# The steps that split the weights, dealt out in four rows over the units of the second batch

## The chip, the cores and the metric

The kernel runs on one core of one Trainium2 chip, as one launch. The metric is the device time of the whole launch in microseconds, as a median of several runs. TensorE does the matmuls and writes to PSUM; ScalarE (ACT), VectorE (DVE) and GpSimd (POOL) do the elementwise work; SyncE (SP) starts nearly all transfers.

## What is computed

Two blocks in a row, all in float32. First a polynomial attention: with two small sketches S1 and S2, every query and key of length 32 becomes 64 products (features), and a feature map takes the place of the softmax. Then a feed-forward block with a gate, over 4352 tokens of width 128 and a hidden width of 1536.

```
a, b    = S1 @ x, S2 @ x                  # 8 numbers each
phi(x)  = all 64 products a_i * b_j       # for q and for k
kv, z   = sum_s phi(k) v,  sum_s phi(k)   # per batch and head
attn    = (phi(q) @ kv) / (phi(q) @ z + 1e-6)
x       = attn, as (4 * 1088 tokens, 4 heads * 32)
out     = (silu(x @ w_gate) * (x @ w_val)) @ w_out
```

## The kernel before

**Blocks and units.** There are four batches of 1088 tokens. Each is cut into three blocks, of 384, 384 and 320 tokens, which gives twelve blocks. The hidden width is cut into twelve slices of 128. A *unit* is one slice for one block: a matmul with a slice of w_gate, a matmul with the slice of w_val, the silu of the first, and its product with the second, which goes to a slot of `hbuf`. Two units later, `down` (L949) multiplies that slot with a slice of w_out and adds it up in PSUM.

**The loop.** The first batch is worked through with hand-written code. The other three run in one loop over y from 0 to 107 near the end of the kernel: nine blocks of twelve units. The second batch is y = 0 to 35. Within a step of the loop the order of issue is: the unit, up to two `down`, then one piece (or two) of the attention work for a later batch (`parts_of`, from the generator `attentions`), then one step of the splitting of the weights (`next(cutting, None)`), then perhaps a step of the splitting of the tokens. No scheduler reorders this: every engine takes its instructions in the order of issue, and waits on semaphores hold the order of data. At y = 12, 36 and 60 a `group` of small matmuls of the attention stands ahead of the unit.

**Plain and split units.** For y up to 37, `unit` uses plain float32 matmuls (L918); each shows as two records in the trace. Later units (`cut_unit`) use three float32r matmuls in the place of one float32 matmul. For them the weights and the tokens have to be split first. For w_val the parts are used from y = 38 on, for w_gate from y = 48 on.

**What the splitting does.** A weight array (wv or wg) is split in four pieces of 128 x 384, and each piece takes four steps, all recorded under L841:

- w1, on ScalarE: the weight, scaled by a little less than one and rounded to float32r
- low, on GpSimd: the weight less w1, in a tile of the tag `sgl`, of which there are six buffers
- wb, on ScalarE: low, times 4096 and rounded
- wd, on GpSimd: w1 less wb

In the profile, the w1 and wb of wg carry the name graw, its wd the name gphq, after the buffers that they use.

**The order before.** `cut_weights` sets the steps of piece c at 3c, 3c + 1, 3c + 3 and 3c + 4, and hands out one such position at each unit, from y = 3 on; it goes on with wg when wv is done. So the ScalarE step wb is issued two units after the GpSimd step low that it reads, followed by the w1 of the next piece. ScalarE has the silu of each unit (L924) in the same queue.

**GpSimd's other work.** In the second batch GpSimd also adds up the key features (`feature_sums`, L526, tile zs): four additions in a row, once for each later batch. They are read at the next group, by small matmuls (L679).

**PSUM.** Units take three banks in turn (g0, g1, g2), two for each unit. The matmul for w_val of a unit takes the bank that held the gate of the unit before, which that unit's silu sets free. The matmul for w_gate takes the bank of the value of two units before, which DVE's product (L935) sets free.

Of the kernel before, what the change touches and what calls it, by code (L numbers as in the profile page):

```python
# [2 lines left out]

# [10 lines left out]
AF = mybir.ActivationFunctionType  # L14
# [6 lines left out]
def kernel(  # L21
# [28 lines left out]
    nc = tc.nc  # L50
# [17 lines left out]
    steps = [(sum(plan[:s]), n) for s, n in enumerate(plan)]  # L68
# [32 lines left out]
    def hold(*tags):  # L101
        for t in tags:
            held.update((place[t], place[t] + 1) if t in "ab" else (place[t],))
# [31 lines left out]
    wg = const.tile([P, NCH, P], FP32, name="wg")  # L135
    wv = const.tile([P, NCH, P], FP32, name="wv")
# [33 lines left out]
    def load_next():  # L170
# [36 lines left out]
        out=ident[:], in_=ident[:], pattern=[[-1, P]], base=0, channel_multiplier=1,  # L207
# [79 lines left out]
    def run(*gens):  # L287
        for g in gens:
            for _ in g:
                pass  # L290
# [521 lines left out]
    BETA = 4096.0  # L812
    CUT = 1.0 - 2.0**-13
# [3 lines left out]
    def whole(ap):  # L817
        return ap.bitcast(FP32)

    def homes(w):  # L820


        if w is wv:
            for c in range(4):
                yield [
                    stage.tile([P, 3, P], F32R, tag=tag, name=name, bufs=6)[:]
                    for tag, name in (("exp", "w1"), ("man", "wb"), (("exp", "man")[c % 2], "wd"))
                ]
        else:
            big = lambda pool, tag, bufs: pool.tile([P, 2, 3, P], F32R, tag=tag, name="g" + tag, bufs=bufs)  # L830
            for c in range(2):
                t = [big(stage, "raw", NRAW), big(stage, "raw", NRAW), big(apool, "phq", 2)]
                for k in range(2):
                    yield [x[:, k] for x in t]

    def cut_weights(w):

        steps = {}

        def put(at, f, **args):  # L840
            steps.setdefault(at, []).append(lambda: f(**args))  # L841

        for c, (w1, wb, wd) in enumerate(homes(w)):
            src = w[:, 3 * c : 3 * c + 3, :]
            low = fpool.tile([P, 3, P], FP32, tag="sgl", name="low", bufs=6)[:]
            w_parts[id(w), c] = (w1, wb, wd)
            sub = dict(op=ALU.subtract)
            put(3 * c, nc.scalar.activation, out=w1, in_=src, func=AF.Copy, scale=CUT)
            put(3 * c + 1, nc.gpsimd.tensor_tensor, out=low, in0=src, in1=whole(w1), **sub)
            put(3 * c + 3, nc.scalar.activation, out=wb, in_=low, func=AF.Copy, scale=BETA)  # L850
            put(3 * c + 4, nc.gpsimd.tensor_tensor, out=wd, in0=whole(w1), in1=whole(wb), **sub)
        for at in sorted(steps):
            for step in steps[at]:
                step()
            yield

    def cut_tokens(i, engine=nc.gpsimd):

        t0, n = blocks[i]
        x = xT[:, t0 : t0 + n]  # L860
        x1, x0, xd = x_parts[i] = [
            apool.tile([P, BW], F32R, tag=tag, name=name, bufs=2)
            for tag, name in (("qb", "x1"), ("dT", "x0"), ("rd", "xd"))
        ]
        nc.scalar.activation(x1[:, 0:n], x, AF.Copy, scale=CUT)
        engine.tensor_tensor(
            out=x0[:, 0:n], in0=x, in1=whole(x1[:, 0:n]), op=ALU.subtract
        )
        yield
        nc.vector.scalar_tensor_tensor(  # L870
            out=xd[:, 0:n], in0=whole(x0[:, 0:n]), scalar=-BETA, in1=whole(x1[:, 0:n]),
            op0=ALU.mult, op1=ALU.add,
        )

    def cut_unit(i, j, both=False):

        t0, n = blocks[i]
        x1, x0, xd = (x[:, 0:n] for x in x_parts[i])
        ws = (wg, wv) if both else (wv,)
        parts = [[x[:, j % 3, :] for x in w_parts[id(w), j // 3]] for w in ws]  # L880
        ds = [bank()[:, 0:n] for _ in ws]
        g = None if both else bank()[:, 0:n]
        for d, (_, _, wd) in zip(ds, parts):
            nc.tensor.matmul(d, wd, xd, start=True, stop=True)  # L884
        if not both:
            nc.tensor.matmul(g, wg[:, j, :], xT[:, t0 : t0 + n], start=True, stop=True)  # L886
        ps = []
        for w1, wb, _ in parts:
            p = bank()[:, 0:n]
            nc.tensor.matmul(p, w1, x1, start=True, stop=False)  # L890
            nc.tensor.matmul(p, wb, x0, start=False, stop=True)  # L891
            ps.append(p)
        sums = []
        for d in ds:
            s = fpool.tile([P, BW], FP32, tag="sgl", name="sum", bufs=6)[:, 0:n]
            nc.scalar.activation(s, d, AF.Copy, scale=-1.0 / BETA)  # L896
            sums.append(s)
        for p, s in zip(ps, sums):
            nc.vector.scalar_tensor_tensor(  # L899
                out=s, in0=p, scalar=1.0 + 1.0 / BETA, in1=s, op0=ALU.mult, op1=ALU.add  # L900
            )
        sg = fpool.tile([P, BW], FP32, tag="sg", name="sg", bufs=3)[:, 0:n]
        nc.scalar.activation(sg, sums[0] if both else g, AF.Silu)  # L903
        slot_of[i, j] = slots.pop(0)
        hj = hbuf[:, slot_of[i, j], :]
        hidden[i, j] = hj
        todo.append((i, j))
        nc.gpsimd.tensor_tensor(out=hj[:, 0:n], in0=sg, in1=sums[-1], op=ALU.mult)  # L908

    def unit(i, j, late=False, between=(None, None)):  # L910


        t0, n = blocks[i]
        g, u = bank(), bank()
        for o, w in ((g, wg), (u, wv)):
            if between[0] and w is wv:
                between[0]()
            nc.tensor.matmul(  # L918
                o[:, 0:n], w[:, j, :], xT[:, t0 : t0 + n], start=True, stop=True
            )  # L920
        sg = fpool.tile(
            [P, BW], FP32, tag="sgl" if late else "sg", name="sg", bufs=6 if late else 3
        )
        nc.scalar.activation(sg[:, 0:n], g[:, 0:n], AF.Silu)  # L924
        slot_of[i, j] = slots.pop(0)
        hj = hbuf[:, slot_of[i, j], :]
        hidden[i, j] = hj
        todo.append((i, j))
        if late:
            if between[1]:  # L930
                between[1]()
            nc.scalar.copy(hj[:, 0:n], u[:, 0:n])
            lates.append((hj[:, 0:n], sg[:, 0:n]))
        else:
            nc.vector.tensor_tensor(  # L935
                out=hj[:, 0:n], in0=sg[:, 0:n], in1=u[:, 0:n], op=ALU.mult
            )
# [5 lines left out]
    def down():  # L943

        i, j = todo.pop(0)
        n = SPLIT if i == LAST else blocks[i][1]
        if j == 0:
            acc[i] = bank("g1" if i == 1 else "acc")
        nc.tensor.matmul(  # L949
            acc[i][:, 0:n],  # L950
            wo[:, j, :],
            hidden[i, j][:, 0:n],
            start=(j == 0),
            stop=(j == NCH - 1),
        )
        if i != LAST:
            hidden.pop((i, j))
            slots.append(slot_of[i, j])
        if j == NCH - 1:
            store(i, n)  # L960
# [47 lines left out]
    for h in range(H):  # L1008
# [13 lines left out]
        out=s12[:, 0:H, :, :],  # L1022
        in0=sTv.unsqueeze(1).to_broadcast([P, H, 2, R]),
        in1=own[:].unsqueeze(2).unsqueeze(3).to_broadcast([P, H, 2, R]),
# [75 lines left out]
    def group():  # L1100
        while ahead[0] != "pe":
            ahead[0] = next(att)
        ahead[0] = next(att, "end")
# [32 lines left out]
    w = ("wg", "wv")  # L1136
# [43 lines left out]
    END = len(line) * NCH  # L1180
    PLAIN, VALUE = 3 * NCH + 2, 4 * NCH
    coming_x = iter(())
    cutting = chain(*(cut_weights(w) for w in (wv, wg)))
    for y in range(END):
        i, j = line[y // NCH], y % NCH
        if y in (NCH, 3 * NCH, 5 * NCH):
            group()
        if y == 3 * NCH:
            oldest[0] = True
            hold("acc")  # L1190
            run(cut_tokens(i, nc.vector))
        if y < PLAIN or y == END - 1:
            unit(i, j)
        else:
            cut_unit(i, j, both=y >= VALUE)
        lag = LAG if y < PLAIN else min(5, END - y + 1)
        for _ in range(2):
            if len(todo) > lag:
                down()
        parts_of(2 if y in (0, 4, 6, 7, 8) else 1)  # L1200
        if 3 <= y:
            next(cutting, None)
        if j == 4 and 3 * NCH < y < END - NCH:
            coming_x = cut_tokens(line[y // NCH + 1])
        if j in (4, 6):
            next(coming_x, None)
# [43 lines left out]
```

## Time and profile before

The median of three runs is 304.58 us (304.5 to 305.13). The profiled execution spans 303.4 us.

| engine | busy us | share of the span | instructions |
|---|---|---|---|
| TensorE, matmul | 288.4 | 95% | 2307 |
| TensorE, weight load | 206.1 | 68% | 2307 |
| VectorE | 200.4 | 66% | 400 |
| ScalarE | 154.6 | 51% | 369 |
| GpSimd | 127.8 | 42% | 144 |

The second batch runs from about 92 to 176 us. The rows of the table are totals over stages with different limits, so what a stage is limited by has to be read from its own waits. A wait is printed as "engine, what it writes, line <- the engine and line that released it". In a timeline the bracket after a row holds the idle time ahead of it and what ended that. "Granted clock" is the share of full speed that TensorE was given in a stretch.

The L841 steps in the trace:

| step | engine | count | mean us | first and last start, us |
|---|---|---|---|---|
| w1 of wv | ScalarE | 4 | 0.51 | 98.1, 117.7 |
| low of wv | GpSimd | 4 | 1.00 | 98.7, 118.8 |
| wb of wv | ScalarE | 4 | 0.52 | 102.0, 119.8 |
| wd of wv | GpSimd | 4 | 1.00 | 102.6, 120.4 |
| w1 of wg | ScalarE | 4 | 0.51 | 130.4, 146.7 |
| low of wg | GpSimd | 4 | 0.99 | 131.0, 147.9 |
| wb of wg | ScalarE | 4 | 0.52 | 134.2, 151.3 |
| wd of wg | GpSimd | 4 | 1.00 | 141.7, 151.9 |

### The profile page before, as it was taken

The page shows a single profiled execution, that of the slowest core. Times are in us where ns is not written, and L with a number is a line of the kernel's source. Part 1 is how long each engine was busy: PE and PEld are TensorE (multiplying, and loading weights), DVE is VectorE, ACT ScalarE, POOL GpSimd, SP SyncE. Part 2 cuts the span into 40 slices and gives each one's busy share as a digit, 9 for nine tenths or more (in the row PEclk, how much of TensorE's full clock was granted, in tenths as well). Part 3 has the DMA queues.
Part 4 walks back from the last instruction along what each step waited for, and adds up shares of the span by engine and source line. Part 5 has one row for each costly group of instructions (what it writes and reads, how often), then busy time and mean ns, then how long its engine had stood idle before and what let it go on. Part 6 is the DMA issues. An engine that isn't in the chain of part 4 may idle for free.

```text
span 303.4 us, 6168 instructions
## 1 busy us (share of the span) xinstructions
PE 288.4 (95%) x2307; PEld 206.1 (68%) x2307; DVE 200.4 (66%) x400; ACT 154.6 (51%) x369; POOL 127.8 (42%) x144
## 2 busy tenths in 40 slices
PE   8899999999999993996899999999999999999995
PEld 7545566657665541753567767787778888888985
DVE  4997988692536982165688348998657666676751
ACT  3566764422103422341422236567868888888870
POOL 3216222174000348029510006777547575576660
PEclk9999999999999996999799999999999999999999
DMA  7554490414411000050001001001001010010101
GB/s 195 161 184 106 123 306 0 149 23 154 101 28 22 0 3 0 22 108 0 0 0 27 3 15 35 0 2 26 0 2 28 2 17 5 0 29 1 23 2 26
DMA packets 26142, 14.63 MB, mean 48 GB/s; under 512 B 18688, under 2 KB 24192, under 8 KB 26112
## 3 DMA queue, kind: packets, MB, share of 16 engines
q1 hardware_dynamic: 25456, 14.13, 18.3%
q8 instruction: 18, 0.29, 0.4%
q10 hardware_dynamic: 656, 0.10, 0.2%
q14 instruction: 12, 0.10, 0.1%
HBM read 11.41 MB, written 2.23 MB: 45 GB/s over the span
## 4 chain that ended last, share of the span: by engine, by line
PE 86%; POOL 5%; DVE 3%; ACT 2%; issue 1%; DMA 1%; SPq 0%; DVEq 0%; POOLq 0%
PE PS L918 29%; PE PS L949 26%; PE PS L884 6%; PE PS L890 6%; PE PS L891 6%; POOL zs L526 4%; PE PS L886 2%; PE PS L771 2%; PE PS L333 2%; PE PS L367 1%; DMA kld<-in_k_dram 1%; PE PS L321 1%; DVE sum L899 1%; PE PS L964 1%; POOL low L841 1%
## 5 line engine op out<-in xcount | busy, mean ns | idle before, releaser
L949 PE MATMUL PS<-hbuf,wo 128*128 128x384 f32 (+2 forms) x288 | 105.9, 464 | 0.4 <-DVE o L978 0.4
L908 POOL TENSOR_TENSOR hbuf<-sg,sum 128x384 f32<-128x384 f32 (+1 forms) x69 | 69.8, 1014 | 67.6 <-ACT sum L896 32.2
L899 DVE SCALAR_TENSOR_TENSOR sum<-PS,sum 128x384 f32<-128x384 f32 (+1 forms) x128 | 62.6, 526 | 29.5 <-ACT sum L896 27.2
L924 ACT ACTIVATE sg<-PS 128x384 f32<-128x384 f32 (+1 forms) x75 | 35.1, 472 | 66.0 <-PE PS L918 62.2
L918 PE MATMUL PS<-xT,wv 128*128 128x384 f32 (+1 forms) x150 | 59.9, 482 | 9.2 <-ACT sg L924 8.9
L949 PEld LDWEIGHTS PS<-hbuf,wo 128*128 128x128 f32 x288 | 53.1, 191 | 18.2 <-issue 1.9
L935 DVE TENSOR_TENSOR hbuf<-sg,PS 128x384 f32<-128x384 f32 (+1 forms) x69 | 36.2, 525 | 40.6 <-PE PS L918 27.7
L918 PE MATMUL PS<-xT,wg 128*128 128x384 f32 (+1 forms) x150 | 59.8, 481 | 0.0
L896 ACT ACTIVATE sum<-PS 128x384 f32<-128x384 f32 (+1 forms) x128 | 53.4, 465 | 5.6 <-PE PS L884 5.2
L918 PEld LDWEIGHTS PS<-xT,wv 128*128 128x128 f32 x150 | 28.6, 194 | 27.9 <-ACT sg L924 10.7
L918 PEld LDWEIGHTS PS<-xT,wg 128*128 128x128 f32 x150 | 27.8, 192 | 18.4 <-issue 1.5
L903 ACT ACTIVATE sg<-sum 128x384 f32<-128x384 f32 (+1 forms) x59 | 29.7, 503 | 17.0 <-DVE sum L899 16.3
L884 PE MATMUL PS<-xd,gphq 128*128 128x384 f32 (+1 forms) x59 | 34.6, 587 | 0.0
L890 PE MATMUL PS<-x,w 128*128 128x384 f32 (+1 forms) x69 | 25.4, 369 | 0.0
L884 PE MATMUL PS<-xd,wd 128*128 128x384 f32 (+1 forms) x69 | 24.7, 357 | 0.0
L891 PE MATMUL PS<-x,wb 128*128 128x384 f32 (+1 forms) x69 | 22.6, 328 | 0.0
L890 PE MATMUL PS<-x,graw 128*128 128x384 f32 (+1 forms) x59 | 19.2, 325 | 0.0
L891 PE MATMUL PS<-x,graw 128*128 128x384 f32 (+1 forms) x59 | 19.1, 324 | 0.0
L884 PEld LDWEIGHTS PS<-xd,wd 128*128 128x128 f32 x69 | 13.1, 190 | 6.8
L884 PEld LDWEIGHTS PS<-xd,gphq 128*128 128x128 f32 x59 | 11.1, 189 | 6.4 <-issue 0.4
L841 POOL TENSOR_TENSOR low<-wv,w 128x384 f32<-128x384 f32 x4 | 4.0, 996 | 27.1 <-ACT w L841 27.1
L890 PEld LDWEIGHTS PS<-x,w 128*128 128x128 f32 x69 | 13.0, 188 | 1.6 <-ACT xT L788 0.3
(129 smaller groups left out, 330.6 us busy)
## 6 DMA issues: line engine op xcount, KB each, us to landing
kld<-in_k_dram SPq DMA_DIRECT2D x4, 544.0 KB, 4.1
vld<-in_v_dram SPq DMA_DIRECT2D x12, 144.0 KB, 5.0
qld<-in_q_dram SPq DMA_DIRECT2D x3, 544.0 KB, 4.0
raw<-in_moe_w_out_dram SPq DMA_DIRECT2D x4, 384.0 KB, 3.8
out_dram<-o SPq DMA_DIRECT2D x28, 48.0 KB, 1.9
raw<-in_moe_w_gate_dram SPq DMA_DIRECT2D x3, 384.0 KB, 3.2
raw<-in_moe_w_val_dram SPq DMA_DIRECT2D x3, 384.0 KB, 3.5
out_dram<-o SPq DMA_DIRECT2D x16, 40.0 KB, 1.7
```

The lines of the kernel that those rows point to most:

```text
L526: add = lambda o, a, b: nc.gpsimd.tensor_tensor(out=o, in0=a, in1=b, op=ALU.add)
L884: nc.tensor.matmul(d, wd, xd, start=True, stop=True)
L890: nc.tensor.matmul(p, w1, x1, start=True, stop=False)
L891: nc.tensor.matmul(p, wb, x0, start=False, stop=True)
L896: nc.scalar.activation(s, d, AF.Copy, scale=-1.0 / BETA)
L899: nc.vector.scalar_tensor_tensor(out=s, in0=p, scalar=1.0 + 1.0 / BETA, in1=s, op0=ALU.mult, op1=ALU.add)
L903: nc.scalar.activation(sg, sums[0] if both else g, AF.Silu)
L908: nc.gpsimd.tensor_tensor(out=hj[:, 0:n], in0=sg, in1=sums[-1], op=ALU.mult)
L918: nc.tensor.matmul(o[:, 0:n], w[:, j, :], xT[:, t0 : t0 + n], start=True, stop=True)
L924: nc.scalar.activation(sg[:, 0:n], g[:, 0:n], AF.Silu)
L935: nc.vector.tensor_tensor(out=hj[:, 0:n], in0=sg[:, 0:n], in1=u[:, 0:n], op=ALU.mult)
L949: nc.tensor.matmul(acc[i][:, 0:n], wo[:, j, :], hidden[i, j][:, 0:n], start=(j == 0), stop=(j == NCH - 1),)
```

## The change

The steps, their engines, their operands and their tiles stay as they are. Only the units at which they are issued are set anew. The steps of each array now stand in four rows of four: w1 of the four pieces at four units in a row, low at the next four, wb eight units after low, and wd four units after wb. The rows of wv begin at y = 2 and those of wg at y = 14, so at y = 14 to 17 the wb of wv and the w1 of wg share a unit, and at y = 18 to 21 the wd of wv and the low of wg. The aim is that no ScalarE step comes up for execution before the GpSimd step that it reads is long done. A table `cutting` from y to a list of steps takes the place of the chained generators.

```diff
-    def cut_weights(w):
-
-        steps = {}
+    def cut_weights(w, at, steps):
...
-            put(3 * c, nc.scalar.activation, out=w1, in_=src, func=AF.Copy, scale=CUT)
-            put(3 * c + 1, nc.gpsimd.tensor_tensor, out=low, in0=src, in1=whole(w1), **sub)
-            put(3 * c + 3, nc.scalar.activation, out=wb, in_=low, func=AF.Copy, scale=BETA)
-            put(3 * c + 4, nc.gpsimd.tensor_tensor, out=wd, in0=whole(w1), in1=whole(wb), **sub)
-        for at in sorted(steps):
-            for step in steps[at]:
-                step()
-            yield
+            put(at + c, nc.scalar.activation, out=w1, in_=src, func=AF.Copy, scale=CUT)
+            put(at + 4 + c, nc.gpsimd.tensor_tensor, out=low, in0=src, in1=whole(w1), **sub)
+            put(at + 12 + c, nc.scalar.activation, out=wb, in_=low, func=AF.Copy, scale=BETA)
+            put(at + 16 + c, nc.gpsimd.tensor_tensor, out=wd, in0=whole(w1), in1=whole(wb), **sub)
...
-    cutting = chain(*(cut_weights(w) for w in (wv, wg)))
+    cutting = {}
...
-        if 3 <= y:
-            next(cutting, None)
+        for w, at in ((wv, 2), (wg, 14)):
+            if y == at:
+                cut_weights(w, at, cutting)
+        for step in cutting.pop(y, ()):
+            step()
```

More of the change, by code (lines that the diff above doesn't have):

```diff
@@ L1 @@
 from contextlib import ExitStack
-from itertools import chain
 import concourse.bass as bass
```

## The prediction

> **What bounds the kernel now.** I read the page first, then the waits, then the timeline around the longest wait. Section 1 has TensorE busy 95% of the span, and part 4 puts 86% of the chain on it. The question is where the other 14% lies, so I asked who waited for whom, all engines, 92 to 180 us (us in total, times, longest):
>
> ```profile
> PE PS L918 <- ACT sg L924: 8.9, 2, 5.4
> ACT wb L841 <- POOL low L841: 8.3, 2, 7.4
> ACT graw L841 <- POOL low L841: 6.4, 2, 5.5
> ```
>
> TensorE waits twice in this batch, 8.9 us, each time for ScalarE's silu (sg). ScalarE in turn waits for a difference (low) on GpSimd. The chain in time order says what stands before it (start, length):
>
> ```profile
> 110.00 2.38 POOL zs L526
> ...
> 114.58 0.72 POOL zs L526
> 115.31 0.95 POOL wd L841
> 116.26 0.96 POOL low L841
> 117.24 0.52 ACT wb L841
> 117.76 0.41 ACT w L841
> 118.18 0.39 ACT sg L924
> 118.60 1.65 PE PS L918 x2
> ```
>
> One chain from GpSimd's four feature sums (zs, 110.0 to 115.3 us) over a wd and a low, to the wb and w1 on ScalarE, to the silu of unit 10, whose PSUM bank the value matmul of unit 11 needs. In the timeline the second case has the same form:
>
> ```profile
> 143.70 0.52 ACT L841 ACTIVATE graw<-low 128x384 fp32r<-128x384 f32 x1 [5.49 <-POOL low L841]
> ...
> 144.54 0.85 ACT L924 ACTIVATE sg<-PS 128x384 f32<-128x384 f32 x2
> ...
> 145.06 0.91 PE L918 MATMUL PS<-xT,wv 128*128 128x384 f32 x2 [3.52 <-ACT sg L924]
> ```
>
> The busy table by stretch (length, TensorE, its weight loads, DVE, ScalarE, GpSimd, granted clock) shows that TensorE also comes back slow:
>
> ```profile
> 92.00:112.40 20.40, 20.40 (x65) 11.82 (x64) 18.84 (x31) 6.96 (x15) 5.32 (x4) 1.00 0.06 9
> 112.40:121.50 9.10, 3.69 (x13) 1.40 (x13) 2.16 (x4) 2.21 (x5) 7.56 (x8) 0.67 0.00 0
> ...
> 127.00:140.30 13.30, 13.30 (x43) 7.90 (x42) 9.24 (x13) 4.77 (x11) 5.29 (x4) 1.00 0.31 68
> 140.30:150.00 9.70, 6.18 (x14) 3.23 (x13) 3.76 (x6) 3.12 (x7) 7.22 (x8) 0.82 0.00 0
> ...
> 156.00:175.60 19.60, 19.60 (x77) 13.41 (x76) 11.97 (x21) 5.25 (x12) 0.00 (x0) 1.00 0.07 12
> ```
>
> Outside the two holes TensorE is busy all the time at clock 1.00, and DVE (second closest) has slack only on average: 18.84 of 20.40, then 9.24 of 13.30, then 11.97 of 19.60.
>
> **What the Trainium skill says.** *PSUM — Partial Sum Buffer*, Engine vs sequencer instructions: the queues of ScalarE, VectorE and GpSimd are strictly first in, first out. The trace agrees: the silu of unit 10 had its matmul by about 111.4 us and ran at 118.08, behind wb. *TensorE: Matmul & The Clock Gate*, What's actually happening: an idle window of some 3.4 us halves the clock, and it takes such a window busy to come back. The trace agrees: clock 0.67 and 0.82 in the holes, and the pair after the first takes 1.65 us where others take 0.81. *SBUF — State Buffer*, Who interferes with whom: a DVE instruction with two SBUF inputs and a GpSimd one that reads SBUF exclude each other. The trace agrees: an L720 product of 0.95 us alone took 2.06 from 136.97, beside the sum that runs from 135.86 for 2.36, and ended 0.8 us after it.
>
> **The change, part by part.** Nothing is removed: 16 ScalarE scalings (0.51 to 0.52 us) and 16 GpSimd subtractions (0.99 to 1.00 us) stay; only their places in the queues move. The rows are: wv's w1 at units 2-5, low 6-9, wb 14-17, wd 18-21; wg's at 14-17, 18-21, 26-29, 30-33. I number units by y; silus at 97.75, 109.36, 128.10, 137.71 and 156.63 us are units 3, 9, 12, 17 and 24.
>
> *First hole.* In units 6-13 ScalarE now has no instruction that reads a GpSimd result, so silus 10 and 11 run when their matmuls are done. The value matmul of unit 11 then starts at 112.39 + 0.645 (pace of a pair: 1.29 us for two on the chain) = 113.03 instead of 118.60: 5.57. From there to the group at 121.46 TensorE took 2.86 us for two pairs, at pace 1.29: another 1.57. Together 7.14 us; the group starts at about 114.3.
>
> *Second hole.* Units 18 to 25 have no such instruction either. Unit 19's value matmul starts at 140.74 + 0.645 = 141.39 instead of 145.06 (3.67); from there to 150.08 five pairs took 5.02 us instead of 3.23 (1.79). Together 5.46 us. The sum is **12.6 us**. I count nothing more for clock: after the first hole L771 and L367 take 1.50 and 1.16 us on the chain, and 1.48 and 1.16 in the undisturbed group at 175.64.
>
> *New waits, and what hides them.* (a) GpSimd's first sum now has low 0 and 1 ahead of it and low 2 and 3 behind. The first two depend on scalings of about 96.7 and 98.6 us and are done by about 100; the sum starts on DVE's last product at 110, as now, and ends at 115.3. Its reader is the group itself (L679), reached at 114.3 + 1.5 + 1.2 = 117.0: a margin of 1.7 us only. (b) wb 2 and 3 at units 16 and 17 need low 2 and 3, done at 115.3 + 2 x 0.96 = 117.2; unit 16's silu is at 135.78 - 7.1 = 128.6: margin 11 us. (c) Behind the second sum (128.7 to 134.6) stand eight subtractions, four wd of wv and four low of wg in turn: 7.7 us, until 142.3. The wb of wg come at units 26 to 29, from 160.13 - 12.6 = 147.5 on; margin 5 us to the end of the whole row. (d) wd of wv is needed at unit 38 (182.25 - 12.6 = 169.7), wd of wg (about 153) at unit 48: no wait. (e) In units 14-17 ScalarE has silu, wb and w1, 1.3 us in a unit of 1.94; units 15, 17 and 19 have that now, with TensorE at full pace in 15. Nothing.
>
> *The lock.* The eight subtractions in units 18-22 meet DVE's L720 (units 18, 20) and the short products of unit 22 (L736, L742), and the four wd at 147.5 to 153 meet L356 of units 25 and 27. Each DVE instruction with two SBUF inputs can wait for one subtraction, 0 to 0.96 us, half as a mean: six such, 0 to 5.8, about 2.9 us. Taken away is one in units 5-7 (L356 at 103.98 took 1.39) and the 0.6 of L720 at 145.51. DVE has 0.4 us of slack in a unit of 1.94 and 0.15 in one of 1.61, and its product may end some 1.9 us late before unit y+2 lacks its PSUM bank. Most is hidden; the skill's lock also can hold back GpSimd, by 0.95 us an encounter, inside the margins of (b) and (c). I charge 0.2 us, with 0 and 2 as ends.
>
> 304.58 - 12.6 + 0.2 = **292.2 us**.
>
> **Rivals.** *The lock makes DVE the bound* between units 18 and 28: for it, weight loads already wait for L935 by 0.36 us at 110.35, so the bank reserve can run out; against it, DVE's 9.24 of 13.30 us. It costs 1 to 2 us: about 293.7. *One hole stays*: the first as a direct wait of the group for zs (margin 1.7 us, so for a full stay GpSimd would have to be 7 us later than worked out), or the second, were the silu there held by DVE rather than the queue. Only the first gone: 304.58 - 7.1 = 297.5; only the second: 299.1. Against both: in the changed order those silus wait for TensorE alone. *Both holes stay in another shape, slower*: silus held by something else, and the lock's mean 2.9 us less the two taken away (0.4 and 0.6) added in full: 304.58 + 1.9 = 306.5. Only the low margin at L679 speaks for it.
>
> **How the numbers follow.** Both holes gone at 292.2 within 1 us: 0.73. Lock as bound, 293 to 294.5: 0.13. A hole kept in whole or part, 295 to 300: 0.07. Better than 291.2, from slack that I don't see in later stages: 0.04. Slower: 0.02; within 0.2%: 0.01. The range 291.2 to 294.5 holds the first two. Faster gathers 0.73 + 0.13 + 0.07 + 0.04 = 0.97.
>
> **What would show it.** Right: TensorE's wait for sg L924 (8.9 us, two times) is absent, granted clock 1.00 from 92 to 156, sums on GpSimd off the chain, silu of unit 10 at about 111.4 and of 12 near 121, the group of unit 36 near 163. The lock: L720 and L356 above 0.95 us, and TensorE waiting for L935. Wrong: L679 or L689 waiting for zs, or ScalarE idle ahead of a wb by over 0.5 us.

## The result, and the profile after

The kernel after takes 292.75 us (median of 4 runs, 292.29 to 292.9), the one before 304.58 us on the same chip (304.5 to 305.13). The ratio is 0.9605, with a 95% interval of 0.9589 to 0.9622: 11.83 us less. The two profiled executions, whose spans are 303.4 and 290.6 us, differ by 12.8 us; the first took 305.07 us, near the slow end of before's runs, the second 292.29, the fastest of after's. What the traces show is that 12.8.

The line numbers have moved: L841 is now L838, the units' matmuls are L911 (was L918), their silu L917 (was L924), DVE's product L928 (was L935), `down` L942 (was L949).

First, who TensorE waited for in the whole run (us in total, times, longest):

```profile
PE PS L225 <- PEq L1230: 0.9, 1, 0.9
PE PS L942 <- DVE o L971: 0.4, 1, 0.4
PE PS L475 <- ACT kvz L1072: 0.4, 1, 0.4
...
PE PS L911 <- DVE wv L270: 0.2, 1, 0.2
PE PS L320 <- issue: 0.2, 1, 0.2
```

The row that led this list before, 8.9 us for the silu, is absent, and no new one stands in its place. The busy table of the kernel after, by stretch (length, TensorE, weight loads, DVE, ScalarE, GpSimd, clock):

```profile
112.40:120.00 7.60, 7.38 (x260) 5.38 (x259) 2.44 (x6) 2.04 (x6) 4.35 (x5) 1.00 0.05 12
...
127.00:137.50 10.50, 10.50 (x34) 6.24 (x33) 8.51 (x13) 4.93 (x12) 8.72 (x7) 1.00 0.03 5
137.50:143.40 5.90, 5.90 (x20) 3.45 (x19) 5.14 (x9) 1.47 (x3) 5.90 (x6) 1.00 0.00 0
143.40:163.00 19.60, 19.60 (x88) 13.42 (x102) 12.81 (x21) 6.89 (x16) 4.29 (x5) 1.00 0.07 12
```

From 92 to 163 us TensorE is busy all the time but for 0.22 us in the group, at clock 1.00. From 137.5 to 143.4 us it is now GpSimd that has no pause, 5.90 of 5.90 us, and TensorE doesn't wait for it. Here is GpSimd's timeline around the two sums; in the bracket, the idle time ahead of the row:

```profile
109.65 2.37 POOL L525 TENSOR_TENSOR zs<-hbuf 128x1024 f32<-128x1024 f32 x1 [9.82 <-DVE hbuf L355]
...
114.25 0.73 POOL L525 TENSOR_TENSOR zs<-zs,hbuf 128x256 f32<-128x256 f32 x1
114.94 1.97 POOL L838 TENSOR_TENSOR low<-wv,w 128x384 f32<-128x384 f32 x2
...
137.89 1.71 POOL L838 TENSOR_TENSOR low<-wg,graw 128x384 f32<-128x384 f32 x1
...
142.66 1.00 POOL L838 TENSOR_TENSOR low<-wg,graw 128x384 f32<-128x384 f32 x1
```

The first sum still starts as DVE's features are done (109.65, before 110.00), and low 2 and 3, those of the third and fourth piece, still stand behind it. But nothing reads these two before 128.85 us. ScalarE's timeline:

```profile
111.39 0.49 ACT L917 ACTIVATE sg<-PS 128x384 f32<-128x384 f32 x1 [1.45 <-PE PS L911]
113.33 0.49 ACT L917 ACTIVATE sg<-PS 128x384 f32<-128x384 f32 x1 [1.45 <-PE PS L911]
...
128.85 0.51 ACT L838 ACTIVATE wb<-low 128x384 fp32r<-128x384 f32 x1
...
147.67 0.52 ACT L838 ACTIVATE graw<-low 128x384 fp32r<-128x384 f32 x1
```

The silus of units 10 and 11 run at 111.39 and 113.33 us, each with 1.45 us of idle time ahead of it, ended by its own matmul. The last low of wg ends at 143.66, and the first wb of wg comes at 147.67.

### The profile page after: what moved, and what is told of

It reads as the page before. It is cut to its first block, busy times and chain, and to the rows that moved or that the text cites. A ratio compares the mean times of both kernels' runs of the same rounds, so it can differ in the third digit from the quotient of the medians.

```text
span 290.6 us, 6170 instructions
## 1 busy us (share of the span) xinstructions
PE 284.5 (98%) x2307; PEld 204.6 (70%) x2307; DVE 200.7 (69%) x400; ACT 154.5 (53%) x369; POOL 130.1 (45%) x144
## 4 chain that ended last, share of the span: by engine, by line
PE 91%; DVE 3%; DMA 1%; issue 1%; ACT 1%; POOL 0%; SPq 0%; DVEq 0%
PE PS L911 32%; PE PS L942 28%; PE PS L877 7%; PE PS L883 7%; PE PS L884 7%; PE PS L879 2%; PE PS L770 2%; PE PS L332 2%; PE PS L366 2%; DMA kld<-in_k_dram 1%; PE PS L320 1%; DVE sum L892 1%; PE PS L957 1%; PE PS L475 1%; PE PS L423 1%
## 5 line engine op out<-in xcount | busy, mean ns | idle before, releaser
L942 PE MATMUL PS<-hbuf,wo 128*128 128x384 f32 (+2 forms) x288 | 104.7, 460 | 0.4 <-DVE o L971 0.4
L917 ACT ACTIVATE sg<-PS 128x384 f32<-128x384 f32 (+1 forms) x75 | 35.4, 473 | 68.5 <-PE PS L911 66.1
L942 PEld LDWEIGHTS PS<-hbuf,wo 128*128 128x128 f32 x288 | 52.5, 189 | 17.6 <-issue 0.7
L911 PE MATMUL PS<-xT,wg 128*128 128x384 f32 (+1 forms) x150 | 59.1, 476 | 0.0
L911 PE MATMUL PS<-xT,wv 128*128 128x384 f32 (+1 forms) x150 | 58.3, 470 | 0.2 <-DVE wv L270 0.2
L928 DVE TENSOR_TENSOR hbuf<-sg,PS 128x384 f32<-128x384 f32 (+1 forms) x69 | 36.1, 524 | 28.6 <-PE PS L911 26.8
L911 PEld LDWEIGHTS PS<-xT,wv 128*128 128x128 f32 x150 | 28.3, 190 | 17.9 <-DVE hbuf L928 0.9
L911 PEld LDWEIGHTS PS<-xT,wg 128*128 128x128 f32 x150 | 27.6, 190 | 18.2 <-issue 1.2
L838 POOL TENSOR_TENSOR low<-wv,w 128x384 f32<-128x384 f32 x4 | 4.7, 1176 | 25.4 <-ACT w L838 25.4
L525 POOL TENSOR_TENSOR zs<-hbuf 128x1024 f32<-128x1024 f32 x2 | 4.7, 2364 | 21.5 <-PE PS L911 11.6
```

The costliest lines, as they stand in the source:

```text
L911: nc.tensor.matmul(o[:, 0:n], w[:, j, :], xT[:, t0 : t0 + n], start=True, stop=True)
L928: nc.vector.tensor_tensor(out=hj[:, 0:n], in0=sg[:, 0:n], in1=u[:, 0:n], op=ALU.mult)
L942: nc.tensor.matmul(acc[i][:, 0:n], wo[:, j, :], hidden[i, j][:, 0:n], start=(j == 0), stop=(j == NCH - 1),)
```

## The experiments

Two theories were tested against one another in most of these. The *queue* theory: a ScalarE step that reads a GpSimd result which is late holds up the silus behind it, and TensorE stands for want of a PSUM bank. The *lock*: what counts is how often GpSimd's subtractions and DVE's two-input products meet. Others are named where they come up. The experiments ran on three chips, with three medians of the kernel before: 306.08 us (e1 to e4), 305.85 (e5 to e8) and 305.05 (e9 to e11). So I compare savings, or kernels of one chip. The kernel after was not run beside e1 to e4.

### e1 and e2: one array's rows at a time

A table gives, for piece c, the units of w1, low, wb and wd.

```diff
+    # e1: wv in four rows; wg at the places of before
+    ROWS = {id(wv): lambda c: (2 + c, 6 + c, 14 + c, 18 + c),
+            id(wg): lambda c: (13 + 2 * c, 14 + 2 * c, 15 + 2 * c, 16 + 2 * c)}
+    # e2: wv at the places of before; wg in four rows
+    ROWS = {id(wv): lambda c: (3 + 2 * c, 4 + 2 * c, 5 + 2 * c, 6 + 2 * c),
+            id(wg): lambda c: (14 + c, 18 + c, 26 + c, 30 + c)}
```

> The kernel after, but with the steps of wg at their places of before (one position at each unit from y = 13). Only the first hole should close. Queue theory (a ScalarE step that reads a late GpSimd result holds up the silus behind it): 304.6 - 7.1 = 297.5 us, between 297 and 298.5; TensorE's wait for sg of 3.5 us at unit 19 is still there, that of 5.4 us at unit 11 is not. Rival, the lock (the gain comes from GpSimd's subtractions no longer meeting DVE's products): the time follows the number of such meetings, no more than 1 us saved, 303.5.

> The kernel after, but with the steps of wv at their places of before (one position at each unit from y = 3), and those of wg in the four rows. Only the second hole should close. Queue theory: 304.6 - 5.5 = 299.1 us, between 298.5 and 300; the wait of 5.4 us at unit 11 is still there and clock falls only there. Rival, the lock: about 303.5. If the two holes are independent, the two savings add up to that of the whole change, 11.8 us.

Measured: e1 297.92 us (ratio 0.9703, 0.9647 to 0.9759), 8.2 less than before; e2 300.86 us (0.9809, 0.9737 to 0.988), 5.2 less. The interval of e2 reaches up to 0.988, so it is faster, but a gain of 2% isn't certain. The forecasts were savings of 7.1 and 5.5 us. e2's time lies outside what was expected and e1's inside, but both were reckoned from a before of 304.6 us, and this chip's is 1.5 us slower. The sum of the two savings is 13.4, with 11.8 to 12.8 us for the whole change in its three comparisons; before's seven runs here range over 3.6 us, so each saving is known to about 2 us. The profiled spans are closer together: 296.1 us (e1) and 298.4 (e2) against 303.4 before, which is 7.3 + 5.0 = 12.3, and 12.8 for both. TensorE's waits, of e1:

```profile
PE PS L912 <- ACT sg L918: 3.5, 1, 3.5
```

and of e2:

```profile
PE PS L912 <- ACT sg L918: 5.4, 1, 5.4
```

Each keeps just the hole whose array stayed at the old places, at its old length. So the holes are independent within this noise, and the rows of each array pay for their own.

### e3: one instruction put back

```diff
-            put(at + 12 + c, nc.scalar.activation, out=wb, ...)
+            put(9 if w is wv and c == 2 else at + 12 + c, nc.scalar.activation, out=wb, ...)
```

> The kernel after with one instruction moved: the wb of the third piece of wv is issued at y = 9, as in the kernel before, and not at y = 16. The low that it reads stands behind the first sum on GpSimd. Queue theory: ScalarE stands from 109.9 until low is done at 115.9, the silu of unit 10 runs at 116.4 in the place of 111.4, TensorE waits some 3.6 us at unit 11 and comes back at a lower clock for some 1.5 us: 292.75 + 5 = 297.8 us, between 296.5 and 298.5. Rival, the order of GpSimd's steps is what counts: nothing on GpSimd moves, so 292.75.

Measured: 297.98 us, some 5 us above the kernel after (292.6 to 293.1 us in its three sets of runs). ScalarE's timeline of e3:

```profile
109.69 0.49 ACT L917 ACTIVATE sg<-PS 128x384 f32<-128x384 f32 x1 [1.45 <-PE PS L911]
116.17 0.52 ACT L838 ACTIVATE wb<-low 128x384 fp32r<-128x384 f32 x1 [5.99 <-POOL low L838]
116.60 0.85 ACT L917 ACTIVATE sg<-PS 128x384 f32<-128x384 f32 x2
```

After the silu of unit 9, ScalarE stands for 5.99 us in front of one wb. Two silus come out in a heap behind it; TensorE waits 3.6 us and has clock 0.81 from 112.4 to 121.5 (columns as in the busy table of the kernel after):

```profile
112.40:121.50 9.10, 5.49 (x95) 2.60 (x97) 2.28 (x5) 1.69 (x5) 4.54 (x5) 0.81 0.00 0
```

GpSimd's order is that of the kernel after, so the cause is the place of one ScalarE instruction in its queue.

### e4 and e9: the sums made shorter, the steps left where they were

```diff
     # e4, for the third and fourth batch
-        add(s[:], rows[:, 0:4, :], rows[:, 4:8, :])
-        add(s[:, 0:2, :], s[:, 0:2, :], s[:, 2:4, :])
-        add(s[:, 0, :], s[:, 0, :], s[:, 1, :])
-        add(s[:, 0, :], s[:, 0, :], rows[:, 8, :])
+        add(s[:, 0, :], rows[:, 0, :], rows[:, 8, :])
     # e9
-        add(s[:], rows[:, 0:4, :], rows[:, 4:8, :])
-        add(s[:, 0:2, :], s[:, 0:2, :], s[:, 2:4, :])
+        add(s[:, 0:2, :], rows[:, 0:2, :], rows[:, 2:4, :])
```

> The kernel before with the key sums of the third and fourth batch cut to one addition of 128 x 256 (0.7 us in the place of 5.3 us); the other seven chunks are left out of these sums. The steps of the splitting stay where they were, ScalarE's wb two units behind low. Queue theory: wb 2 is then free at about 112.7 us, so the first hole shrinks to about 1 us without a fall of the clock, the second goes: about 293 us, between 292.5 and 294. Rival, the distance of two units is too short in itself: 304. Rival, the lock: at most 2 us less, 302.5.

> The kernel before with the key sums of the third and fourth batch made 2.4 us shorter (the first, widest addition left out, and with it five of the nine chunks). The steps of the splitting stay where they were. Queue theory: each hole gets 2.4 us shorter, the first from 5.4 to about 3.0 us, the second from 3.5 to about 1.1 us. If that were all, 4.8 us less, 301. But the second then is too short for a fall of the clock (1.8 us more back), and the first perhaps: 7 to 8 us less, about 298, and granted clock 1.00 after the second. Rival, the clock falls with any hole: 301.

Both leave chunks out of the sums, e4 seven of the nine and e9 four (not five, as its expectation says), so their outputs are not the kernel's; only their times are read here.

Measured: e4 293.71 us, 12.4 less than before, with a wait for the silu of 0.9 us left. This is the gain of the whole change with not one splitting step moved: the sums are what the late low stood behind.

Measured, e9: 295.4 us, 9.7 less, so more than expected. TensorE's waits of e9:

```profile
PE PS L923 <- ACT sg L929: 1.3, 1, 1.3
...
PE PS L923 <- DVE hbuf L940: 0.8, 1, 0.8
```

There are two reasons. The clock stayed at 1.00. The waits fell from 8.9 to 2.1 us, which is 6.8 of the 9.7; the other 2.9 I put down to TensorE's slow return, which no longer happens. And the holes are shorter than expected: the first is 1.3 us, not 3.0, and the second, of which 1.1 were to stay, is all but gone. I had overlooked that the short sum doesn't read DVE's last features. It starts earlier, at 108.98 us in the place of 110.00, and though its additions then take longer, it ends 2.8 us sooner (112.48, before 115.30) and not 2.4. The larger part of what the first hole lost is that TensorE comes to it later: its last matmul ahead of it starts at 113.65 in the place of 112.39, chiefly since it has already stood 0.8 us at unit 10. For that, DVE's timeline of e9:

```profile
108.14 2.95 DVE L356 TENSOR_TENSOR hbuf<-kabs 128x512 f32<-128x512 f32 x3
111.01 0.54 DVE L940 TENSOR_TENSOR hbuf<-sg,PS 128x384 f32<-128x384 f32 x1
```

The same three products take 1.89 us in the kernel after. Here they run beside the sum (two SBUF inputs on DVE, reads on GpSimd) and take 1.06 us longer; DVE's product is late, and TensorE waits 0.8 us for a bank. That fits the lock, reaching TensorE in a unit where DVE had no slack.

### e5 and e11: the kernel after again

> The kernel after, once more, on the same chip as the next three. All theories: 292.3 to 292.9 us on a chip like the first. Its runs lie within 0.6 us, while those of before spread by 3 us or more, if the clock's return after a hole differs from run to run and a kernel without holes has no such return.

> The kernel after on the same chip, to compare the other two with: 292.3 to 293.2 us.

Measured: 293.09 us (292.28 to 294.43, 6 runs) and 292.58 us (292.49 to 292.81, 4 runs), which are 12.8 and 12.5 less than before. The first spread wider than the 0.6 us that I expected: one run of six, with clock 0.994, took 294.43, and without it the range is still 1.15 us. Ten of before's runs on that chip go from 304.1 to 307.4 us (an eleventh took 308.73). They sort themselves by granted clock: 304.1 and 304.9 us at 0.989 and 0.987, 305.4 to 306.1 at 0.983, 306.9 to 307.4 at 0.977 or 0.978. So runs of one program differ by some 3 us with the clock. That the clock is lost at the holes can be read only in the profiled executions: in that of before, it is under 1.00 from 112.4 to 127 and from 140.3 to 150 us and nowhere else. For the other runs it is inferred.

### e6 and e7: the distance

```diff
     # e6; in e7 the new places are at + 6 + c and at + 10 + c
-            put(at + 12 + c, nc.scalar.activation, out=wb, ...)
-            put(at + 16 + c, nc.gpsimd.tensor_tensor, out=wd, ...)
+            put(at + 8 + c, nc.scalar.activation, out=wb, ...)
+            put(at + 12 + c, nc.gpsimd.tensor_tensor, out=wd, ...)
```

> The kernel after with wb four units behind low in the place of eight (and wd still four behind wb). Queue theory: wb 2 of wv comes up at unit 12, about 121 us, and low 2 is done at 115.9; wb 3 of wg at unit 25, about 146 us, and its low is done at 143.7. Nothing waits: the time of the kernel after, within 0.5 us. Rival, it is the distance in units as such that counts and a gain grows with it: half of the gain, about 298.5.

> The kernel after with wb two units behind low, the distance of the kernel before, but with GpSimd's low steps still in a row of their own. Queue theory: wb 2 at unit 10 stands until about 115.9, the silu of unit 11 runs at 116.4 and the copies of the group behind wb 3 at 117.4 in the place of 115.8, so the group's key matmuls start some 1 us late; in the second row the ScalarE waits are below 1 us and inside the bank's slack. 1 to 1.5 us above the kernel after: about 294. Rival, the distance: 304. Rival, the order of GpSimd's steps alone: the time of the kernel after.

Measured: e6 292.95 us (292.62 to 293.19), e7 293.38 us (293.06 to 293.84), beside 293.09 for the kernel after. Four units do as well as eight, as forecast. With two units nearly the whole gain is there as well, where 1 to 1.5 us more than the kernel after were forecast. But two units are not the distance of the kernel before, as is said ahead of the prediction and in the expectations of e4 and e7. There it is one unit: `cut_weights` passes over positions at which nothing is to be done, so low at 3c + 1 and wb at 3c + 3 come in units next to each other (`4 + 2 * c` and `5 + 2 * c` in the table of e2). The runs that have that distance are e4, which keeps it for every piece and has the whole gain, and e3, which goes back to it for one piece and loses 5 us. Of e7, one wait of ScalarE and what came of it on TensorE:

```profile
ACT wb L838 <- POOL low L838: 4.1, 1, 4.1
...
PE PS L332 <- ACT xT L787: 0.9, 1, 0.9
```

ScalarE stands for 4.1 us in front of wb 2, even so. But at unit 10, one unit later than in e3, the group of small matmuls comes before the next silu whose bank is wanted, and takes up most of it. Only 0.9 us is left. The medians differ by less, 0.3, but e5's runs scatter by more than that, and its profiled execution has 0.9 us of idle time in the group that nothing explains (see the end), which e7's has not. So it isn't the distance in units, as e4 shows. It is whether the step comes up after its data are there, and if not, what waits behind it.

### e8: the margin of the group

```diff
         add(s[:, 0, :], s[:, 0, :], s[:, 1, :])
+        for _ in range(4):
+            add(s[:, 3, :], s[:, 2, :], rows[:, 8, :])
         add(s[:, 0, :], s[:, 0, :], rows[:, 8, :])
```

> The kernel after with the key sums of the third and fourth batch made 2.9 us longer (one addition of 128 x 256, 0.72 us, done four times more into unused space). The first sum then ends at 117.9 us and not 115.0, and the group needs it at 116.7. Queue theory, with the sums' only near reader being the group's matmuls (L678): TensorE waits 1.2 us there, the second sum has no near reader; 1.1 to 1.5 us above the kernel after. Rival, other readers of GpSimd's row are near as well (wb of wg, wd): 3 us or more. Rival, no reader is near: no change.

Measured: 294.19 us (294.12 to 294.24), 1.1 above e5. TensorE's waits of e8 (L686 is L678 of the kernel after):

```profile
PE PS L686 <- POOL zs L525: 1.1, 1, 1.1
...
PE PS L950 <- DVE o L979: 0.7, 2, 0.4
```

The margin is there and is as narrow as worked out: in the kernel after, the sum ends at 114.98 and L678 starts at 116.72. But that the median is just 1.1 us higher is in part luck, and the longer second sum isn't free. The silus of e8 run 1.0 us later than in the profile of the kernel after at unit 22 (141.11 and 140.07), and 1.9 later from unit 27 on (150.81 and 148.89). In between, GpSimd's eight subtractions, pushed back by the sum, run until 149.05 in the place of 143.66, beside other products of DVE; TensorE's weight loads wait 0.9 us for DVE's product and 0.8 us for its transpose, and the last row above has one wait for a transpose more than the kernel after (0.4, once). So the profiled execution is 1.9 us longer than that of the kernel after (292.5 and 290.6). e5, with which the medians are compared, scatters over 2.2 us, and its own profiled execution has 0.7 us more of an idle time in the group that nothing explains (see the end), which hides a part.

### e10: more for DVE to meet

```diff
-            put(at + 16 + c, nc.gpsimd.tensor_tensor, out=wd, ...)
+            for _ in range(2):
+                put(at + 16 + c, nc.gpsimd.tensor_tensor, out=wd, ...)
```

> The kernel after with each of the eight wd subtractions on GpSimd done twice (into the same place), eight more instructions of 1.0 us, where DVE has its two-input products. The queue theory, with the wait of DVE for GpSimd inside the slack: no change, within 0.5 us of the kernel after on a like chip (292.3 to 293.2). Rival, the lock as the near bound (1 to 2 us in the prediction for the eight there are): 1.5 us or more above it, with TensorE waiting for L928. Also the row behind the second sum grows by 4 us; low of wg is still done by about 148 us, ahead of wb 3 at 152.5.

Measured: 293.32 us (293.14 to 295.21) beside 292.58 of e11: 0.7 more, between the two theories. Of e10, the waits for DVE from 92 to 165 us:

```profile
PEld PS L912 <- DVE hbuf L929: 1.1, 3, 0.5
...
PEld PS L943 <- DVE o L972: 0.8, 1, 0.8
...
PE PS L943 <- DVE o L972: 0.3, 1, 0.3
```

Weight loads wait 1.1 us for DVE's product, where the kernel after has 0.4 us, and 0.8 us for a transpose, where TensorE itself shows 0.3. Against the kernel after, the silus are 0.5 us late at unit 22 (140.55 and 140.07) and 1.2 at unit 27 (150.06 and 148.89): 0.7 us is lost in these units, as much as the medians differ by. The queue theory's forecast, no change within 0.5 us, missed that. Eight more subtractions use up DVE's slack, as the longer second sum of e8 did. The kernel after stands just within it.

## Why the prediction was right

**The cause.** Right. The queue carries it (e3), the sums stand ahead of the late low (e4), and the holes are two separate ones (e1, e2).

**First hole**, forecast 7.14 us. The silu of unit 12 went from 128.10 to 120.78, which is 7.32; the units before were 0.10 later in this execution than in that of before, so 7.4. The waits and the two slow pairs were right. The step that was short is "I count nothing more for clock". The L771 of the undisturbed group, which I took for comparison, has another width (192 against 288 columns in a block). The chain of the kernel after has the right one:

```profile
114.58 1.16 PE PS L770 x36
115.74 1.16 PE PS L366 x72
```

1.16 us for L770, where before it took 1.50 after the hole: 0.3 us more that went to the clock.

**Second hole**, forecast 5.46 us: from unit 14 (131.97 to 124.65, 7.32) to unit 22 (152.86 to 140.07, 12.79) it is 5.47.

**The lock**, charged with 0.2 us, measured none. From unit 22 to the group's copy at unit 36 (177.18 to 164.39) the shift stays 12.79. DVE did pay: one L719 took 1.36 us and one L355 1.72, with 0.95 for each alone, and the short instructions of unit 22 some 0.7 us in all. That is 1.8 us, against 2.9 as the mean of six encounters (the L719 of unit 18 ran before the row of subtractions began). So one half of the lock's sign came, products of DVE above 0.95 us, and the other did not, TensorE waiting for them. Without e8 and e10 one could say that it doesn't matter; with them, that it was close.

**The waits** (a) to (e) were free as forecast. The row of eight subtractions ended at 143.7 and not 142.3, since GpSimd's steps also take longer beside DVE's products (one low took 1.71 us). (a) was the only one of the five that was near, and e8 showed it; e8 and e10 showed that DVE's reserve was near too.

**The size.** 12.4 us forecast, 11.83 as the difference of medians at first, 12.8 and 12.5 with e5 and e11, 12.8 between the profiles. The 0.55 us by which the time was missed is within what differs between executions, and that it came so close is in part luck. The holes gave 12.9 us in the traces where 12.6 were worked out, and the lock took nothing where 0.2 were charged. Against that, the working read its savings from an execution of 305.07 us and took them off the median of 304.58.

**How much of it was waiting.** Of the 12.9 us in the traces, TensorE's waits for the silu were 8.9 us, and the starts of the two matmuls were put off by another 0.3 (5.57 and 3.67 against waits of 5.41 and 3.52). The slow return is the rest: 1.57 + 1.79 + 0.3, 3.7 us. From the medians of the third chip of the experiments an estimate is 12.47 - 8.9 = 3.6.

## What to carry to other kernels

In a queue that runs in order, a step that nobody is in a hurry for can stop one that everybody needs. Issue it only when its data are sure to be there: look up what else stands ahead of the *producer* on its own engine, not how many steps lie between the two in the program. When you cost such a hole, add what TensorE loses when it comes back, and compare it with a piece of work of the same shape.

## What the runs showed of the hardware

Holes of 0.8 to 1.3 us (e4, e7, e8, e9) left the granted clock at 1.00. Holes of 3.5, 3.6 and 5.4 us (e1, e3, e2) did not: it was 0.93 from 127 to 150 us, 0.81 and 0.78 from 112.4 to 121.5. No run has a hole between 1.3 and 3.5 us. The two in the kernel before cost 3.7 us on top of the waits.

The prediction did not foresee that this would make the slower kernel's runs scatter so: 304.1 to 307.4 us over a clock of 0.989 to 0.977 on the chip of e5, with 292.3 to 294.4 for the kernel without holes. The clock is lost in steps. One less the granted clock, times the span, estimates how much each run lost. It is 0 to 0.6 us, 1.8 to 2.1, 3.3 to 4.0, 5.2, or 6.7 to 7.0 us in every run whose clock is on record: steps of about 1.7 us. e1 lost one step, e3 one and in one run two, e2 two, the kernel before two, three or four. One run each of e5 and e10 lost a step too, without such a hole in their profiles; where is not known, since only one execution of each was profiled. Nor does all lost clock cost time: before's profiled execution lost 5.2 us of it and came back 3.7 us slower.

*TensorE: Matmul & The Clock Gate* of the Trainium skill, section What's actually happening, gives half the clock and a window of about 3.4 us, and says that the window runs freely, not from the start of the kernel. Half the clock for 3.4 us would lose 1.7 us, which agrees with the steps, and that one program loses two to four of them agrees with a window that runs freely. No run here shows where a window begins.

Left open: the group shows 0.2 to 0.9 us of idle time on TensorE that no release in the trace explains (L320, "issue"). It is absent in e7 and e8, where TensorE waits earlier in the group, and under 0.1 us in e2. In the profiles TensorE's wait for the first keys (kT, near the start) also differs, from none to 1.2 us. I didn't test what sets either. They are among the reasons why medians that differ by less than a microsecond prove little without the traces.
